# Splitting the third block's transposes around the scale sums of rows 6 to 8

## Chip, cores, metric

One core of one Trainium2 chip. The metric is the device time of one execution in microseconds (us). A profiled execution also has a span, from its first to its last instruction, which is some 1.7 us shorter. All runs that are compared are of the fast state with a granted clock of 1.0, unless the text says otherwise.

## The reference

One block of a diffusion transformer (DiT) on two batches of 256 tokens, width D = 1152, two heads of 576. What matters here is its head:

```python
mod = (_silu(c) @ w_mod).reshape(B, 6, 1, D)
shift_a, scale_a, gate_a, shift_m, scale_m, gate_m = [mod[:, i] for i in range(6)]
h = _layernorm(x, axis=-1) * (1 + scale_a) + shift_a
qkv = (h @ wqkv).reshape(B, N, 3, H, Dh)
```

Attention, the output projection and a gated MLP follow; the change doesn't touch them.

## The kernel before

The 512 tokens are four blocks of 128, numbered t = 0 to 3 in the code: "first block" is t = 0, "third block" is t = 2. VectorE normalises each block; PE transposes it in nine k-tiles (128 columns each); a k-tile is scaled by `1 + scale_a` on its way to the K projection. The scales are sums on PE over nine rows of k-tiles of `w_mod`, three rows per DMA. PE runs the units in the order of the program:

```python
def xn_T(t, ka=0, kb=KT):                      # PE: transposes of block t, k-tiles ka to kb
    ...
    for kt in range(ka, kb):
        tr(xslot(b, kt)[...], XN[:, t, kt * 128:(kt + 1) * 128], IDENT)

def sca(k0, k1):                               # PE: scale sums of rows k0 to k1, first four k-tiles
    for kt in range(k0, k1):
        mod_f0(kt)                             # two columns, bank of the first k-tile
    for kt in range(k0, k1):
        mod_kt(WSC, kt, 0, "sca_%d" % kt, (1, KC))
...
warm(7, "b")                                   # matmuls that only keep PE busy
for n, behind in ((1, "bn_ln1_1_1"), (1, "aggr_ln1_1"), (2, "veps_ln1_1"), (2, "rstd_ln1_1")):
    warm(n, behind, behind)
xn_T(1)
sca(0, 3)
warm(1, "d")
sca(3, 6)
warm(1, "f", "aggr_ln1_2")
xn_T(0)
sca(6, 9)
xn_T(2, 0, 8)
hk(0, 0)                                       # VectorE: scaled k-tile 0 for K, needs all nine rows
sc1a(0, 1, 1); sc1a(1, KC); hk(1, 0)
xn_T_copy(0, 4, 8, "act"); xn_T_copy(0, 8, 9, "act")    # ScalarE: frees two PSUM banks
...
k_first(0)                                     # PE: K projection, k-tile 0, eight matmuls
k_first(1)
xn_T(2, 8, 9)
xn_T(3)
```

## Time and profile before

| | before |
|---|---|
| time, first three runs | 244.01 us (243.94 to 244.44) |
| profiled span | 242.6 us |
| PE busy, share of the span | 98% |
| first block's transposes, sums of rows 6 to 8, third block's transposes (first matmul) | 10.19, 10.69, 11.01 us |
| K projection, k-tile 0 (first matmul); fourth block's transposes | 11.55; 13.40 us |

PE is the bound, so the change is worth what it opens or closes in PE's waits from the first block's transposes to the fourth block's. Such a wait shows as a late start of a weight load (PEld). The prediction shows and reads the lines.

### The profile page before, as it was taken

The numbers are of one execution on the slowest core, as the hardware profiler recorded it, in microseconds if no ns is written. First come the engines' busy times: TensorE is split into PE (matmuls) and PEld (weight loads), VectorE is DVE, ScalarE is ACT, GpSimd is POOL, SyncE is SP. The second block draws the span as 40 slices with busy tenths as digits, with TensorE's granted clock in tenths as the row PEclk, the third lists the DMA queues.
The fourth block names the chain that finished last, engine by engine and source line by source line (L and its number), as shares of the span: only waits on it lengthen the run. The fifth ranks groups of instructions, "written<-read, shape, count | busy, mean of one in ns | idle before, by whom it ended". The sixth has DMA issues, their size and how long they took to land.

```text
span 242.6 us, 3989 instructions
## 1 busy us (share of the span) xinstructions
PE 238.3 (98%) x1717; PEld 146.4 (60%) x1727; DVE 120.0 (49%) x216; ACT 66.9 (28%) x136; POOL 21.7 (9%) x39
## 2 busy tenths in 40 slices
PE   7999999999999999999999999999999999999996
PEld 2688854557667666898444444444565665665664
DVE  3824379596988799789999600000012222211112
ACT  4730350345424207983233332222000000000000
POOL 1500000000021186400000000020000000000000
PEclk9999999999999999999999999999999999999999
DMA  6999999999994999999943488002000000000001
GB/s 237 330 383 394 388 392 389 397 412 408 390 355 138 349 385 393 390 320 394 329 145 87 165 301 331 0 16 85 0 16 19 16 16 19 16 16 16 19 17 32
DMA packets 29995, 51.57 MB, mean 213 GB/s; under 512 B 1431, under 2 KB 15643, under 8 KB 29979
## 3 DMA queue, kind: packets, MB, share of 16 engines
q1 hardware_dynamic: 29536, 50.14, 57.8%
q0 software_dynamic: 416, 1.19, 1.6%
q8 instruction: 13, 0.21, 0.4%
q14 instruction: 3, 0.02, 0.0%
q10 hardware_dynamic: 27, 0.00, 0.0%
HBM read 50.14 MB, written 1.19 MB: 212 GB/s over the span
## 4 chain that ended last, share of the span: by engine, by line
PE 98%; issue 0%; POOL 0%; DVE 0%; POOLq 0%
PE psum L688 96%; PE psum L691 2%; POOL arena L713 0%; DVE arena L1289 0%; DVE arena L1290 0%; POOL arena L712 0%; POOL arena L719 0%; POOL arena L717 0%; POOLq L1351 0%
## 5 line engine op out<-in xcount | busy, mean ns | idle before, releaser
L688 PE MATMUL psum<-arena 128*128 128x384 bf16 (+9 forms) x1628 | 235.0, 310 | 2.0 <-POOL arena L713 1.5
L688 PEld LDWEIGHTS psum<-arena 128*128 128x128 bf16 (+1 forms) x1638 | 141.1, 97 | 91.8 <-issue 4.7
L1081 DVE SCALAR_TENSOR_TENSOR arena<-arena 128x1152 f32<-128x1152 bf16 x32 | 44.7, 1413 | 0.6
L1289 DVE TENSOR_TENSOR arena<-psum,arena 128x384 f32<-128x384 f32 (+2 forms) x13 | 6.9, 527 | 68.3 <-PE psum L688 68.3
L1197 ACT ACTIVATE arena<-psum 128x512 bf16<-128x512 f32 (+1 forms) x44 | 22.4, 519 | 42.7 <-PE psum L688 42.7
L683 ACT ACTIVATE arena<-psum 128x512 bf16<-128x512 f32 (+6 forms) x37 | 19.5, 549 | 39.8 <-PE psum L688 38.5
L685 DVE CAST arena<-psum 128x512 bf16<-128x512 f32 (+3 forms) x13 | 8.1, 639 | 11.5 <-PE psum L688 11.5
L669 POOL DMA_DIRECT2D dit_scratch<-arena x3 | 1.8, 616 | 116.4 <-DVE arena L685 59.6
L1165 POOL TENSOR_TENSOR arena<-arena 128x384 f32<-128x384 f32 x12 | 10.9, 912 | 10.9 <-DVE arena L1164 9.3
L1108 DVE CAST arena<-psum 72x32 bf16<-72x32 f32 x1 | 0.2, 188 | 21.3 <-PE psum L688 21.3
L741 DVE BATCH_NORM_STATS2 arena<-arena 128x6 f32<-128x384 f32 (+1 forms) x18 | 9.5, 551 | 0.1
L1170 ACT ACTIVATE arena<-arena 128x1152 bf16<-128x1152 f32 x4 | 5.3, 1343 | 11.3 <-DVE arena L1169 11.3
L1164 DVE TENSOR_TENSOR arena<-psum,arena 128x384 f32<-128x384 f32 x12 | 6.5, 550 | 1.3 <-PE psum L688 1.2
L691 PEld LDWEIGHTS psum<-arena 128*128 128x128 bf16 (+1 forms) x89 | 5.9, 98 | 2.1 <-DMA arena<-in_c_dram 0.8
L691 PE MATMUL psum<-arena 128*128 128x128 bf16 (+1 forms) x89 | 7.1, 219 | 0.1
L1290 DVE TENSOR_TENSOR arena<-arena 128x384 bf16<-128x384 f32 (+2 forms) x13 | 6.9, 527 | 0.4
L1187 ACT ACTIVATE arena<-psum,arena 128x128 bf16<-128x128 bf16 x16 | 6.0, 455 | 1.5 <-PE psum L691 0.9
L1184 DVE TENSOR_SCALAR arena<-psum,arena 128x128 bf16<-128x128 bf16 x20 | 5.4, 336 | 1.9 <-PE psum L691 1.9
L1085 DVE STREAM_TRANSPOSE arena<-arena 128x1152 f32<-128x1152 f32 x4 | 5.5, 1368 | 0.0
L1088 DVE TENSOR_REDUCE arena<-arena 128x36 f32<-128x1152 f32 x4 | 5.4, 1346 | 0.0
L1011 ACT ACTIVATE arena<-psum,arena 128x256 bf16<-128x256 f32 x8 | 3.7, 472 | 1.3 <-PE psum L688 0.9
L745 POOL TENSOR_TENSOR arena<-arena 128x1 f32<-128x1 f32 x6 | 3.6, 596 | 1.6 <-DVE arena L744 1.6
(48 smaller groups left out, 45.3 us busy)
## 6 DMA issues: line engine op xcount, KB each, us to landing
arena<-in_w_fc_dram SPq DMA_DIRECT2D x9, 1152.0 KB, 7.1
arena<-in_w_fc_dram SPq DMA_DIRECT2D x4, 2592.0 KB, 17.4
arena<-in_wqkv_dram SPq DMA_DIRECT2D x18, 288.0 KB, 9.7
arena<-in_w_mod_dram SPq DMA_DIRECT2D x3, 1728.0 KB, 20.5
arena<-in_w_mod_dram SPq DMA_DIRECT2D x3, 864.0 KB, 13.0
arena<-in_w_mod_dram SPq DMA_DIRECT2D x9, 288.0 KB, 11.1
arena<-in_wqkv_dram SPq DMA_DIRECT2D x1, 2592.0 KB, 16.9
arena<-in_wo_dram SPq DMA_DIRECT2D x1, 2592.0 KB, 24.4
```

Source lines behind the costliest of these rows:

```text
L683: act(c_act(n), lambda e: e.activation(out=dst, in_=src, func=ACTF.Copy), [src], [dst], name)
L685: dve(c_dve_psum16(n) if psum16 else c_dve_psum32(n), lambda e: e.tensor_copy(dst, src), [src], [dst], name)
L688: S.instr(lambda e: e.matmul(o, lhsT=l, rhs=r, start=st, stop=sp, **kw), reads=[l, r], writes=[o])
L691: S.instr(lambda e: e.transpose(o, i_, idn), reads=[i_, idn], writes=[o])
L741: dve(550, lambda e, s=s, o=o: e.bn_stats(out=o, in_=s), [s], [o], "bn_%s_%d" % (tag, ci))
L1081: dve(1270, lambda e, w=w, s=s, acc=acc: e.scalar_tensor_tensor(out=acc, in0=w, scalar=s, in1=acc, op0=ALU.mult, op1=ALU.add), [w, s, acc] ...
L1164: dve(550, lambda e, o=o, ga=ga, x1c=x1c: e.tensor_tensor(out=x1c, in0=o, in1=ga, op=ALU.mult), [o, ga], [x1c], "wo_t1_%d_%d" % (t, ci))
L1165: S.op("pool", 930, lambda e, xs=xs, x1c=x1c: e.tensor_tensor(out=x1c, in0=x1c, in1=xs, op=ALU.add), reads=[x1c, xs], writes=[x1c], name=" ...
L1187: act(440, lambda e, o=o, dst=dst, s1=s1, s2=s2: e.activation(out=dst, in_=o, func=ACTF.Identity, scale=s1, bias=s2), [o, s1, s2], [dst], ...
L1197: act(c_act(ntok), lambda e: e.activation(out=dst, in_=o, func=ACTF.Gelu_apprx_tanh), [o], [dst], "gelu_%d_%d" % (f, tok0))
L1289: dve(c_dve_psum32(w), lambda e, o=o, gm=gm, t1=t1: e.tensor_tensor(out=t1, in0=o, in1=gm, op=ALU.mult), [o, gm], [t1], "fc2_t1_%d_%d" % ( ...
L1290: dve(c_dve_32(w), lambda e, t1=t1, x1c=x1c, ost=ost: e.tensor_tensor(out=ost, in0=t1, in1=x1c, op=ALU.add), [t1, x1c], [ost], "fc2_out_%d ...
```

## The change

The intent, as far as the order tells it: let four transposes of the third block run ahead of the sums of rows 6 to 8, so that PE has something to do if the weights of those rows are late.

```diff
         warm(1, "f", "aggr_ln1_2")
         xn_T(0)
+        xn_T(2, 0, 4)
         sca(6, 9)
-        xn_T(2, 0, 8)
+        xn_T(2, 4, 8)
         hk(0, 0)
```

## The prediction

> **What bounds the kernel now.** I read the page first: the chain that ended last, then the share by engine. The tensor engine (PE) carries the whole span.
>
> ```profile
> span 242.6 us, 3989 instructions
> PE 238.3 (98%) x1717; PEld 146.4 (60%) x1727; DVE 120.0 (49%) x216; ACT 66.9 (28%) x136; POOL 21.7 (9%) x39
> ...
> PE 98%; issue 0%; POOL 0%; DVE 0%; POOLq 0%
> ```
>
> The change moves four of PE's 1717 matmuls by a few places in its order. It can therefore alter the time only by opening or closing an idle stretch of PE. The 98% can't show that, because ends of matmuls are modelled: a matmul that waits looks busy. So I read the timeline of the stretch concerned and worked with the starts of the weight loads (PEld), which do show a wait. Here is 9.7 to 14 us, where L691 is a transpose, L688 a matmul, L807 the scaling of a k-tile for the K projection, L797 the copy of the scale sums, L683 the copy of transposed tiles out of PSUM.
>
> ```profile
> 9.77 0.58 DVE L762 TENSOR_SCALAR arena<-arena 128x1152 bf16<-128x1152 bf16 x1
> ...
> 9.98 0.70 PEld L691 LDWEIGHTS psum<-arena 128*128 128x128 bf16 x9
> ...
> 10.63 0.42 PEld L688 LDWEIGHTS psum<-arena 128*128 128x128 bf16 x12
> 10.69 0.46 PE L688 MATMUL psum<-arena 128*128 128x2 bf16 x12
> 10.89 1.30 ACT L683 ACTIVATE arena<-psum 128x1024 bf16<-128x1024 bf16 x2 [1.36 <-PE psum L688]
> 10.98 0.46 PEld L691 LDWEIGHTS psum<-arena 128*128 128x128 bf16 x8
> 10.99 0.35 DVE L807 TENSOR_SCALAR arena<-psum 128x256 bf16<-128x256 bf16 x1 [0.65 <-PE psum L688]
> 11.01 0.61 PE L691 MATMUL psum<-arena 128*128 128x128 bf16 x8
> 11.27 0.22 DVE L797 COPY arena<-psum 128x2 f32<-128x2 f32 x2
> 11.52 0.35 DVE L807 TENSOR_SCALAR arena<-psum,arena 128x256 bf16<-128x256 bf16 x1
> 11.52 0.56 PEld L688 LDWEIGHTS psum<-arena 128*128 128x128 bf16 x6
> ...
> 12.24 1.04 PEld L688 LDWEIGHTS psum<-arena 128*128 128x128 bf16 x10 [0.15 <-ACT arena L683]
> ...
> 13.29 0.65 PEld L691 LDWEIGHTS psum<-arena 128*128 128x128 bf16 x10
> ```
>
> In PE's order this is: nine transposes of the first block (9.98), twelve scale sums of rows 6 to 8 (10.63), eight transposes of the third block (10.98), then the K projection, first k-tile (11.52) and second. Two things to see. PE has no hole from 9.98 to 11.44, but it has short ones at 11.52 and at 12.24. And the hole at 11.52 has no releaser, although VectorE's first scaling (10.99 + 0.35 = 11.34) had long ended. The row of the kernel's explicit waits in this stretch names it: two stand-alone waits on PE, at 11.4 and 12.4.
>
> ```profile
> L471 PEldq EVENT_SEMAPHORE  x2: 51/51/51, 11.4 to 12.4; - x2
> ```
>
> L471 is the wait on a DMA semaphore. The issues of the weights for k-tile 0 (issued 5.97) and k-tile 1 (issued 6.35), each asked for in its own narrow window, take this long to land:
>
> ```profile
> arena<-in_wqkv_dram SPq DMA_DIRECT2D x1, 288.0 KB, 5.4
> ...
> arena<-in_wqkv_dram SPq DMA_DIRECT2D x1, 288.0 KB, 6.0
> ```
>
> 5.97 + 5.4 is 11.4 and 6.35 + 6.0 is 12.4 (the trace's landing records: 11.42 and 12.39). So the first k-tile of the K projection starts when its weights land, not when VectorE is done, and the second k-tile again starts when its weights land. Between them, at 12.24, PE waits for ScalarE's second copy (10.89 + 1.30 = 12.19), since that copy frees the PSUM bank for the fourth pair of output chunks. After 12.5 us I compared each matmul's start with its column count: PE is dense nearly to the end: its holes are at most 0.13 us (the one at 20.10, behind VectorE, is of this kind), and the larger skips are single matmuls whose record is missing.
>
> **What the Trainium skill says.** "TensorE: Matmul & The Clock Gate", "Wait — 56ns, not 53.3ns?", gives 55.6 ns start to start for warm 128-column matmuls and a floor of about 25 ns for small ones. The trace agrees: the third block's eight transposes start from 11.01 to 11.39, seven steps, 55 ns each; the twelve two-column sums step by 26 ns. Switching between the two kinds adds nothing (57 ns after the last transpose, 28 ns after the last sum). "Perfetto Trace Analysis", "Sequencer-only Instruction (DRAIN, etc)", says that the reported start is the moment all semaphores are satisfied. That is how I read the wait at 11.447: the landing at 11.42 released it. The same page, "Tensor Engine Instruction (MATMUL, LD_WEIGHTS)", says the end of a matmul is an estimate; hence my use of starts.
>
> **The change part by part.** Instructions removed or added: none. The eight transposes of the third block stay eight, in the same banks (four in one bank, four in another, so the split falls on the bank border). Moved: four of them, from behind the twelve sums to ahead of them. PE's own work is the same to the nanosecond: 9x55 + 4x55 + 12x26 + 4x55. Their input is ready: the third block's normalised rows are written by 9.77 + 0.58 = 10.35, and the transposes would start at 10.63.
>
> What moves is what waits for the sums. They start 4 x 55 = 0.22 us later:
>
> 1. VectorE's first scaling reads a sum of row 8, the third of the twelve. It goes from 10.99 to 11.21 and ends at 11.57 instead of 11.35. The copies go from 11.27 to 11.49, the second scaling from 11.52 to 11.74 (end 12.09).
> 2. PE's first k-tile needs that scaling. Where PE truly waits for VectorE, at 20.10, the load starts some 0.05 us after the scaling's end (19.755 + 0.291 = 20.05). So its load would go from 11.52 to about 11.62: 0.10 us later, not 0.22, because 0.12 us were hidden behind the weights' landing.
> 3. That delay then runs into the 12.24 wait. Before: six matmuls of 256 columns (109 ns a step) from 11.555 would reach the seventh at 12.21, which waits until 12.243. After a real stall a matmul start follows the load at once, so the first starts at about 11.63 and the rest step from there after a first step of 0.12: the seventh is due at about 12.29. ScalarE's copy isn't moved (it waits for the first block's transposes alone) and ends at 12.19, so this wait vanishes. What is left of the delay: about 0.05 us; the eighth starts at 12.40 instead of 12.362.
> 4. The second k-tile starts at 12.529, as its weights land at 12.39 and the stand-alone wait and the load cost 0.14. PE would be ready for it at 12.40 + 0.11 = 12.51, and VectorE's second scaling at 12.09 + 0.05 = 12.14. So it starts at 12.529 again. Remaining delay: 0.
> 5. Everything later on PE is unchanged. The block 3 normalisation on VectorE goes from 11.79 to 12.01 (end 12.58), but its transposes start at 13.29. ScalarE's scalings wait for its own copies (12.07), not for the sums (the last copied by about 11.71).
>
> Is there a gain at the other side? The first four transposes exist 0.3 us earlier, but their consumers on VectorE and ScalarE (14.16) wait for the fourth block's transposes, at 13.29. Gain 0.
>
> Sum: +0.22 at the sums, -0.12 behind the first landing, -0.05 behind the copy, -0.05 behind the second landing: 0.0 us. Predicted 244.0, the time before.
>
> **The rivals.** *The delay stays.* If the weights land earlier in the runs that are timed than in the profiled one, steps 2 and 4 hide less. But step 3 still holds, as ScalarE's copy waits for none of the K weights: some 0.05 us would be left, 244.06. The full 0.22 (244.23) would need ScalarE's copy to be earlier too, and nothing in the profile speaks for that.
>
> *The transposes fill a DMA wait.* This is probably the intent. The scale weights of rows 6 to 8 were issued at 2.81 and took 7.7 to land, 10.5; PE comes to them at 10.63. There is a margin of some 0.13 us, so in this profile no wait to fill. If they landed 0.3 us later, PE would wait 0.17 us before and nothing after. But the K weights are behind them in the same stream and would be later too, and the second k-tile would again start at its landing. An earlier start of the sums is worth nothing then: 244.0 again, at best some 0.1 less if only that one transfer slips.
>
> *The build orders something else differently.* VectorE's and ScalarE's order is fixed by hand only up to the K projection; after that the kernel's own list scheduler picks by modelled times. A model shift of 0.2 us could swap two instructions in the softmax or the evacuations. PE is dense there and both engines have slack (VectorE 49%, ScalarE 28% busy), so I give it some 5% to matter, and then by 0.3 us either way: 243.7 to 244.3.
>
> **Range and chances.** The mechanism says 0.0 to +0.05 us. The three runs before spread from 243.94 to 244.44, ten times that, so the range is the spread of a median of such runs, with a little for the third rival: 243.6 to 244.5. Two per cent is 4.9 us; no part of this reaches a tenth of it. I leave 1% in all for the unforeseen.
>
> **What would show it right or wrong.** In the changed profile: four transposes loaded at 10.63 and four after the sums; VectorE's first scaling at 11.21; the first K load at 11.6 with VectorE's L807 as releaser, where before there was none; the wait for ScalarE's L683 at 12.24 gone or shorter; the second stand-alone wait still at 12.4; the next transposes at 13.29 as before; and the span within 0.1 us if nothing else changed. Wrong would be: the transposes at 13.29 moved by 0.1 us or more, a new wait on the second k-tile for VectorE, or another order of VectorE or ScalarE instructions after 25 us.

## The result, and the profile after

| | before | changed |
|---|---|---|
| time, six runs each | 244.07 us (243.83 to 244.44) | 244.26 us (244.23 to 244.30) |
| ratio | | 1.0007 (95%: 0.9994 to 1.002) |
| profiled span | 242.6 us | 242.6 us |

A ratio is the mean time of one kernel's fast runs over that of the other's of the same rounds, so it isn't quite the ratio of the medians quoted. Two things don't fit the prediction's picture: the medians are 0.19 us apart, and the changed kernel's six runs lie within 0.07 us, while those of the kernel before spread over 0.6 us.

The page of the changed kernel first; it answers to the first lines of the prediction.

```profile
span 242.6 us, 3999 instructions
...
PE 238.9 (98%) x1727; PEld 146.7 (60%) x1727; DVE 120.0 (49%) x216; ACT 67.0 (28%) x136; POOL 21.3 (9%) x39
```

The ten instructions more are no work: matmul records were missing from the first trace. The timeline of the stretch, changed kernel (start us, duration us, engine, line, operation; in brackets the idle time before and what ended it):

```profile
9.79 0.58 DVE L762 TENSOR_SCALAR arena<-arena 128x1152 bf16<-128x1152 bf16 x1 [0.30 <-POOL arena L745]
...
10.01 0.93 PEld L691 LDWEIGHTS psum<-arena 128*128 128x128 bf16 x13
...
10.89 0.42 PEld L688 LDWEIGHTS psum<-arena 128*128 128x128 bf16 x12
10.92 1.30 ACT L683 ACTIVATE arena<-psum 128x1024 bf16<-128x1024 bf16 x2 [1.69 <-PE psum L691]
...
11.24 0.23 PEld L691 LDWEIGHTS psum<-arena 128*128 128x128 bf16 x4
11.25 0.36 DVE L807 TENSOR_SCALAR arena<-psum 128x256 bf16<-128x256 bf16 x1 [0.87 <-PE psum L688]
...
11.66 1.64 PEld L688 LDWEIGHTS psum<-arena 128*128 128x128 bf16 x16 [0.18 <-DVE arena L807]
...
13.31 0.65 PEld L691 LDWEIGHTS psum<-arena 128*128 128x128 bf16 x10
```

As predicted there are 13 transposes, then the sums, then four transposes; the first K load waits for VectorE's L807; the wait for ScalarE (12.24 before) is gone; and the fourth block's transposes stand at 13.31 instead of 13.29. The stand-alone waits on DMA semaphores, however, moved:

```profile
L471 PEldq EVENT_SEMAPHORE  x2: 51/51/51, 11.1 to 12.3; - x2
```

The K weights landed at 11.03 and 12.00 us here, not at 11.42 and 12.39, so they hid nothing in this execution. To compare executions I use the **stretch**: from the first matmul of the first block's transposes to the first matmul of the fourth block's, on PE. It is 13.400 - 10.188 = 3.212 us before and 13.418 - 10.220 = 3.198 us after. These two profiles thus show no loss, and don't explain 0.19 us.

### The profile page after: what moved, and what is told of

Read it like the earlier page. It is cut to its first block, busy times and chain, and to the rows that moved or that the text cites. A ratio compares the mean times of both kernels' runs of the same rounds, so it can differ in the third digit from the quotient of the medians.

```text
span 242.6 us, 3999 instructions
## 1 busy us (share of the span) xinstructions
PE 238.9 (98%) x1727; PEld 146.7 (60%) x1727; DVE 120.0 (49%) x216; ACT 67.0 (28%) x136; POOL 21.3 (9%) x39
## 4 chain that ended last, share of the span: by engine, by line
PE 99%; POOL 0%; DVE 0%; issue 0%; POOLq 0%
PE psum L688 96%; PE psum L691 2%; POOL arena L713 0%; DVE arena L1290 0%; DVE arena L1291 0%; POOL arena L712 0%; POOL arena L719 0%; POOL arena L717 0%; POOLq L1352 0%
## 5 line engine op out<-in xcount | busy, mean ns | idle before, releaser
L688 PE MATMUL psum<-arena 128*128 128x384 bf16 (+7 forms) x1638 | 235.7, 311 | 1.5 <-POOL arena L713 1.5
L741 DVE BATCH_NORM_STATS2 arena<-arena 128x6 f32<-128x384 f32 (+1 forms) x18 | 9.5, 551 | 0.1
```

What stands on the lines that cost most here:

```text
L688: S.instr(lambda e: e.matmul(o, lhsT=l, rhs=r, start=st, stop=sp, **kw), reads=[l, r], writes=[o])
L741: dve(550, lambda e, s=s, o=o: e.bn_stats(out=o, in_=s), [s], [o], "bn_%s_%d" % (tag, ci))
```

## The experiments

All kernels but the three named below gave a correct result. Compared instruction by instruction, the changed kernel has the order of the kernel before on VectorE, ScalarE, GpSimd and the DMA queue; PE differs in the moved transposes alone. That removes the prediction's third rival (another order from the list scheduler) without a run.

### A control: the same kernel twice

No edit.

> The kernel before, unchanged, as a control: how much do two profiles and two sets of times of one kernel differ? I measure the stretch from the first transpose of the first block to the first transpose of the fourth block on PE (before: 10.19 to 13.40, 3.21 us; changed kernel: 10.22 to 13.42, 3.20 us). My theory (the landings of the K weights differ from run to run, by some 0.4 us between the two profiles, and the change has no part in that): ratio 1.000, and the stretch lies between 3.15 us (weights early, ScalarE's copy decides) and 3.21 us (weights as late as in the first profile). Rival (the change itself made the weights land earlier): the first K weights land again at 11.4 us, and the stretch is again 3.21.

Measured: 244.05 us (243.66 to 244.15), ratio 1.0001 (0.9987 to 1.0014). But the profiled span is 241.93 us, 0.6 us shorter than the first profile of the same kernel (242.55), and the stretch 12.777 - 9.620 = 3.157 us. The whole shift of 0.6 us exists before the first transposes. The weight loads of the first profile at the warm-up matmuls:

```profile
7.32 0.15 PEld L688 LDWEIGHTS psum<-arena 128*128 128x128 bf16 x1 [0.28 <-DVE arena L741]
7.74 0.55 PEld L688 LDWEIGHTS psum<-arena 128*128 128x128 bf16 x3 [0.28 <-issue]
8.41 0.70 PEld L691 LDWEIGHTS psum<-arena 128*128 128x128 bf16 x9
```

And of the control:

```profile
5.61 0.15 PEld L688 LDWEIGHTS psum<-arena 128*128 128x128 bf16 x1 [0.28 <-issue]
6.04 1.04 PEld L688 LDWEIGHTS psum<-arena 128*128 128x128 bf16 x5 [0.28 <-issue]
...
8.00 0.51 PEld L691 LDWEIGHTS psum<-arena 128*128 128x128 bf16 x9 [0.49 <-DVE arena L762]
...
9.42 0.69 PEld L691 LDWEIGHTS psum<-arena 128*128 128x128 bf16 x9
10.09 0.39 PEld L688 LDWEIGHTS psum<-arena 128*128 128x128 bf16 x12
10.44 0.45 PEld L691 LDWEIGHTS psum<-arena 128*128 128x128 bf16 x8
10.88 0.35 PEld L688 LDWEIGHTS psum<-arena 128*128 128x128 bf16 x4
```

(L741 is VectorE's statistics of a block, L762 its write of a block's normalised rows.) The loads one by one, 0.43 us apart, are warm-up matmuls on a half-rate clock; from 7.74 in the first profile, but from 6.04 in the control, they step by 0.22. "TensorE: Matmul & The Clock Gate", "What's actually happening", says that the clock is released after a free-running window of about 3.4 us, at a point that varies from run to run. The profiles agree: their clock records put the release between 4.92 and 7.81 us. I call a release early where PE has finished its warm-ups before VectorE has written the second block's rows, and late otherwise. With a late release PE is still busy with warm-ups when VectorE has the second block ready, and its transposes start at 8.6; with an early one PE waits for VectorE (0.49 us in the control) and they start at 8.0. From there on PE is 0.6 us earlier, **but VectorE is not**. It writes the third block's rows (the L762 after that) by 10.39 in the control and by 10.35 in the first profile. (Over all kept profiles these rows are written between 10.35 and 10.64 us, with either kind of release: later where the input landed later, 10.39 for a landing at 4.58, 10.63 for one at 4.82.) Both profiles that the prediction and its check rested on had a late release.

The first K weights landed at 10.78 in the control, in an unchanged kernel: the change has no part in their landing.

### Doses: four again, eight, two transposes ahead

```diff
-        xn_T(0)
+        xn_T(0); xn_T(2, 0, 4)                # four_again: the change, line numbers kept
         sca(6, 9)
-        xn_T(2, 0, 8)
+        xn_T(2, 4, 8)
```

In `two_ahead` the split is at k-tile 2, in `eight_ahead` all eight go ahead of the sums.

> The changed kernel (its two calls on one line, so that line numbers stay those of the kernel before). Theory: the delay of 0.22 us at the sums is nearly all hidden, the first K load waits for VectorE and comes 0.05 us after its end, the wait for ScalarE's second copy at 12.24 is gone, stretch 3.19 to 3.21 us whatever the landings, ratio 1.000. Rival (the delay stays in full): stretch 3.43 and ratio 1.001, as the 0.19 us between the medians suggests.

> All eight transposes of the third block ahead of the sums, twice the dose. Theory: the sums and VectorE's first scaling come 0.44 us later than before (scaling 11.43 to 11.79), the first K load at 11.84, and now the 0.3 us that this is late exceed what ScalarE's copy (0.05) and the second landing (0.06) hide: stretch 3.40 us, span and time 0.2 us longer (ratio 1.0008). Rival (the position of the transposes doesn't matter, VectorE is never waited for): stretch 3.21, ratio 1.000. Rival (the delay is proportional): twice whatever the four cost.

> Two transposes ahead, half the dose. Theory: VectorE's scaling comes 0.11 us later and ends at 11.46, PE's first K load at about 11.52, where it was before: no new wait. Stretch 3.15 to 3.21 us, ratio 1.000. If the delay were passed on in proportion, half of what the four cost.

| | time us | ratio | stretch us |
|---|---|---|---|
| four_again | 244.27 (244.17 to 244.33) | 1.0008 (0.9995 to 1.0021) | 3.563 |
| eight_ahead | 244.49 (244.28 to 244.86) | 1.0018 (1.0005 to 1.0030) | 3.786 |
| two_ahead | 244.23 (243.99 to 244.73) | 1.0009 (0.9996 to 1.0023) | 3.414 |

All three expectations of the stretch failed: 3.19 to 3.21, 3.40, 3.15 to 3.21. The doses don't start from zero either: even two transposes cost 0.26 us of stretch against the control. The loads of four_again say why:

```profile
9.55 0.66 PEld L691 LDWEIGHTS psum<-arena 128*128 128x128 bf16 x9
10.58 0.23 PEld L691 LDWEIGHTS psum<-arena 128*128 128x128 bf16 x4 [0.36 <-DVE arena L762]
10.76 0.41 PEld L688 LDWEIGHTS psum<-arena 128*128 128x128 bf16 x12
11.11 0.23 PEld L691 LDWEIGHTS psum<-arena 128*128 128x128 bf16 x4
11.53 1.64 PEld L688 LDWEIGHTS psum<-arena 128*128 128x128 bf16 x16 [0.19 <-DVE arena L807]
```

and, of the same kernel, VectorE's write of the third block's rows:

```profile
9.94 0.58 DVE L762 TENSOR_SCALAR arena<-arena 128x1152 bf16<-128x1152 bf16 x1
```

The clock was released early here (at 5.01). PE has finished the first block's transposes and comes to the moved ones 0.36 us before VectorE has written their rows (9.94 + 0.58 = 10.52). PE runs in order, so the sums, whose weights have landed (10.08), wait behind them. In the kernel before, the sums go first and this wait of PE doesn't exist.

### The transposes in the same place, with rows that are ready

```diff
-        xn_T(0); xn_T(2, 0, 4)
+        xn_T(0); xn_T(2, 0, 4, 1)             # reads the second block's rows: a wrong result on purpose
```

> The changed order, but the four moved transposes read the second block's rows, which are ready since 8 us (a wrong result on purpose; number, kind and place of the instructions as in the changed kernel). New theory: when PE's clock is released early, PE reaches the moved transposes before VectorE has written the third block's rows and waits 0.36 us for them, with the sums stuck behind. Then this kernel has no such wait: stretch 3.20 us (3.157 of the unchanged kernel plus what is left of the 0.22 us), against 3.56 of four_again, and times like the kernel before (ratio 1.0002, spread as wide as before's 0.4 us, lowest run near 243.7). Rival (the cost is the place of the transposes, whatever they read): stretch 3.56, ratio 1.0008, all runs between 244.2 and 244.3.

Measured: 244.10 us (243.88 to 244.61), ratio 1.0001 (0.9988 to 1.0013), stretch 13.055 - 9.857 = 3.198 us, with an early release (5.12). The thirteen transposes run without a hole:

```profile
9.31 0.41 PEld L688 LDWEIGHTS psum<-arena 128*128 128x128 bf16 x13 [0.41 <-DMA arena<-in_w_mod_dram]
9.64 0.93 PEld L691 LDWEIGHTS psum<-arena 128*128 128x128 bf16 x13
10.53 0.42 PEld L688 LDWEIGHTS psum<-arena 128*128 128x128 bf16 x12
...
11.29 1.64 PEld L688 LDWEIGHTS psum<-arena 128*128 128x128 bf16 x16 [0.18 <-DVE arena L807]
```

The stretch is the expected 3.20 and not the rival's 3.56, and the times spread again, by 0.7 us. The lowest run, 243.88, isn't quite at the 243.7 that I had named. So the place of the transposes as such doesn't cost 0.41 us. The test is weaker than planned, though: in this execution PE waited 0.41 us for the scale weights of rows 3 to 5 (the load at 9.31) and came to the moved transposes only at 10.36, and VectorE wrote the third block's rows at 10.37. Even with these rows PE would have waited only some 0.07 us, an estimate from these numbers. That it is the wait for the rows that costs rests on the traces that show this wait (four_again above, early_four and trim_four below): there the stretch grows by the length of the wait.

### K weights early: does a landing hide the delay?

```diff
-            for k0, k1 in ((0, 3), (3, 6), (6, 9)):
+            for k0, k1 in ((0, 3), (3, 6), (6, 9))[:2 + (ka > 0)]:
```

The first-chunk sums of rows 6 to 8 take rows 3 to 5 (a wrong result). `early_four` adds the change.

> The order of before, with the K weights early: the first load of the scale weights' rows 6 to 8 (384 KB) is left out and sums 6 to 8 of the first chunks take rows 3 to 5 instead (a wrong result on purpose; it passes the check of races and memory). All later loads move up by about 1 us, so the first K weights land near 10.4 and the second near 11.4. Theory: the first K load comes right behind the last transpose (step 57 ns instead of 162), then ScalarE's two copies are waited for, the second k-tile follows at once; stretch 3.15 us.

> The same early K weights with the change (wrong result on purpose, as in early_before). Theory: the landings can't hide anything now, only ScalarE's copy does: stretch 3.19 us, 0.04 us more than early_before of the same call. Rival (the delay of 0.22 us, or its visible 0.1, was hidden by the landings alone): 0.10 to 0.22 us more. Rival (no delay at all): the same stretch.

Measured: early_before 243.61 us (243.53 to 243.82), stretch 3.156, the first two K weights landed at 9.77 and 10.43, even earlier than expected; early_four 244.16 us (244.12 to 244.18), stretch 3.563. The first is what the theory said, and it is also the control's stretch, so in an early-release execution of the kernel before the landings decide nothing. The second isn't: 0.41 us more instead of 0.04, again with 0.36 us of waiting for L762 ahead of the moved transposes. All four runs of one are 0.30 to 0.65 us above all four of the other. Not all of that need be the change: in the two profiles VectorE's rows differ too (10.35 in early_before, 10.63 in early_four), as the input landed at 4.18 and 4.82 us.

### Two warm-up matmuls fewer

If the release of the clock makes the kernel before spread, and VectorE pins the changed one, then a shorter warm-up queue should help the former alone.

```diff
-        for n, behind in (..., (2, "veps_ln1_1"), (2, "rstd_ln1_1")):
+        for n, behind in (..., (2, "veps_ln1_1")):
```

> The kernel before without the last two warm-up matmuls (those behind the second block's reciprocal root); correct result. If a late release of PE's clock is what makes the kernel before spread (the warm-up matmuls still take 0.43 us each and the first transposes start at 8.6 instead of 8.0), then the queue ends 0.4 us earlier in those runs: the slow ones (244.3 to 244.4) fall to 243.9 to 244.2, the fast ones stay at 243.7; ratio 0.999. Rival (the later landings of the K weights bound such runs anyway): ratio 1.000. Risk: the clock is released one window later and the runs get slower by up to 1.7 us.

> The changed kernel without the same two warm-up matmuls; correct result. New theory: it is pinned by VectorE's third block whatever PE does before, so an earlier PE gains nothing: 244.2 to 244.3 as four_again, spread 0.15 us, ratio 1.0008, and the wait of the moved transposes for VectorE's L762 is there. Rival (the change only costs where the clock comes early): it falls with trim_before.

Measured: trim_before 243.84 us (243.67 to 244.09) against 244.13 us (243.73 to 244.47), ratio 0.9987 (0.9975 to 0.9999); trim_four 244.25 us (244.02 to 244.32), ratio 1.0002 (0.9990 to 1.0014), with the wait in its trace:

```profile
10.69 0.23 PEld L691 LDWEIGHTS psum<-arena 128*128 128x128 bf16 x4 [0.27 <-DVE arena L762]
```

trim_before came out as the new theory said. trim_four did in part: the wait is there and the median is as expected, but the ratio is 1.0002 instead of 1.0008, and the runs spread by 0.30 us instead of 0.15. trim_before is the one correct version whose median lies below both kernels, by 0.3 us; its interval just excludes 1, which for one of thirteen comparisons is weak. Its profile had an early release (4.92; stretch 3.156), so what it does in a late one is inferred from its times, not seen; the danger of a release one window later didn't show in five runs.

### Rows 6 to 8 late: the case that the change is meant for

```diff
+                if k0 != 3 or ka: continue    # the first K weights go ahead of the scale weights of rows 6 to 8
+                dma(WK[:, 0, :], wqkv_v[:, 0, D:2 * D], P * D * 2, "ld_wk0", run=2304)
```

> The order of before, with the scale weights of rows 6 to 8 late: the first K weights (288 KB) are issued ahead of them, after the input has landed, so these rows land near 11.4 instead of 10.5 and PE has a real wait ahead of the sums, the case the change is meant for. Correct result. Theory: PE waits from 10.64 to 11.45 at the sums, then transposes to 12.2, first K load at 12.2, stretch about 3.78 us.

> The change on top of late_before: four transposes now lie in the wait. Theory: the K projection can't start before the sums, their copy through VectorE's scaling and its signal, about 0.67 us from the first sum to the first K load; before, the sums and eight transposes took 0.76 us. So of the 0.22 us moved into the wait only 0.1 us is gained: stretch 3.67 us. Rival (the transposes fill the wait in full): 0.22 us less than late_before, 3.56. Rival of the prediction (nothing is gained, as the next landing decides): the same 3.78.

> late_before once more, as its first profile fell in an execution with a throttled clock (0.993) and its three other runs (244.46 to 244.98) overlap those of late_four (244.26 to 245.0). Theory: PE waits at the sums for the rows 6 to 8 (landing 10.8 to 12.1), and the change can gain at most 0.1 us there: 244.75, less than 0.2 us over late_four's 244.59. Rival (the transposes fill the wait in full): 0.3 us over late_four or more.

Inconclusive. The landing of rows 6 to 8 scattered: 12.09 us in late_before, 11.35 in late_before_again, and 10.83 in late_four, where PE came to the sums at 10.89 and had nothing to wait for (stretch 3.198, as the changed kernel without the edit). late_before_again did wait, and its stretch of 3.761 us is close to the 3.78 expected of late_before. The fast runs at full clock are 244.46 to 244.98 (late_before), 243.77 to 245.07 (late_before_again) and 244.26 to 245.00 (late_four): they overlap. (The ratios, 1.0050, 1.0059 and 1.0022, compare with the unedited kernel, and the first two mix in the executions at half rate named below.) So whether the split gains where PE really waits for these rows stays open, and the expected 0.1 us isn't shown. late_before_again allows an estimate: its sums were 0.74 us late, for which the line fitted to the changed order below gives a stretch of 3.72 us, so the split would have saved some 0.04 us of its 3.761.

One thing came out beside it. In late_before PE waited 1.88 us for the rows, and its clock fell to half. The windows of that kernel (from and to in us, length, busy us of PE, PEld, DVE, ACT and POOL with counts, granted clock, DMA share, GB/s):

```profile
10.00:12.00 2.00, 0.43 (x8) 0.26 (x5) 0.57 (x2) 1.30 (x2) 0.87 (x1) 0.98 1.00 283
12.00:13.00 1.00, 0.86 (x18) 0.86 (x19) 0.53 (x4) 0.00 (x0) 0.00 (x0) 0.50 1.03 375
...
15.00:16.00 1.00, 1.00 (x9) 0.87 (x8) 0.00 (x0) 0.00 (x0) 0.00 (x0) 0.84 1.07 376
```

From 11.9 to 15.3 us PE ran at half rate. That execution (246.94 us) and three of late_before_again's (246.54 to 246.89, clock 0.993) are left out above.

## Why the prediction was right, and where it was not

The time was right: 244.0 predicted, 244.26 measured, range 243.6 to 244.5. The mechanism was half right. "Delay" below is how much longer it is from the first block's first transpose to the first sum than the 0.50 us of the kernel before.

| kernel | release of the clock us | delay of the sums us | stretch us |
|---|---|---|---|
| before, first profile | 7.76 | 0 | 3.212 |
| before, control | 6.19 | 0 | 3.157 |
| early_before | 6.0 to 6.3 | 0 | 3.156 |
| trim_before | 4.92 | 0 | 3.156 |
| changed, first profile | 7.81 | 0.22 | 3.198 |
| four_ready | 5.12 | 0.22 | 3.198 |
| late_four | 7.71 | 0.22 | 3.198 |
| two_ahead | 5.6 to 5.8 | 0.44 | 3.414 |
| trim_four | 6.0 to 6.4 | 0.49 | 3.469 |
| four_again | 5.01 | 0.59 | 3.563 |
| early_four | 7.01 | 0.59 | 3.563 |
| eight_ahead | 5.65 | 0.81 | 3.786 |

(Where the trace has no clock record, the release lies between the last warm-up step of 0.43 us and the first shorter one.) Every kernel of this table with a delay fits one line: stretch = 3.157 + delay - 0.18 us, within 5 ns. So the head of the kernel has 0.18 us of slack behind the sums, and what exceeds it is paid in full.

- **Steps 1 and 2** held: the sums came 0.22 us later in the profile of the changed kernel, and the first K load waited for VectorE's scaling and came at 11.66 (11.62 predicted).
- **Step 3** held: the wait for ScalarE's copy vanished, and "some 0.05 us" were to remain; 3.198 - 3.157 = 0.041 us remained.
- **Step 4**, the landing that hides the rest, holds for the first profile alone. In that execution it had stretched the kernel before by 3.212 - 3.157 = 0.055 us. In the control and in the changed kernel's profile the weights landed earlier and hid nothing.
- **The step that failed** is the sentence ahead of step 1: "Their input is ready: the third block's normalised rows are written by 9.77 + 0.58 = 10.35, and the transposes would start at 10.63." That margin of 0.28 us was one execution's. PE's arrival moves by 0.6 us with the release of its clock, and VectorE's rows don't move with it. With an early release the moved transposes wait for them, the delay is 0.59 us instead of 0.22, and 0.41 us of stretch is paid against the control. four_ready, which has ready rows, pays 0.04 (though its PE also came later, as said above).
- **The spread** of 243.94 to 244.44 was taken for noise, and part of it is not. To set VectorE's own shifts aside, count from the end of its write of the second block's rows to the fourth block's first transpose. With a late release this is 5.48 us in both orders (the two first profiles). With an early one it is 4.80 to 4.88 us in the order before (control, early_before, trim_before), but 5.20 us in the changed order (four_again, early_four and trim_four, within 1 ns). So an early release saves 0.6 to 0.7 us in the order before and only 0.28 us in the changed one, where VectorE's rows then decide; with a late one PE comes to the moved transposes 0.29 us after these rows would let it go (10.72 against 10.43). The difference in the medians, 0.19 us both times, fits a loss in the executions with an early release, but the timed ratios (intervals from 0.9994 and 0.9995 up) don't show it. Nor is the small spread of the changed kernel explained: its eleven runs (first six and four_again) all lie between 244.17 and 244.33, but those of eight_ahead and two_ahead, which wait for the same rows, spread over 0.58 and 0.74 us.
- **Rivals.** "The delay stays" named the right size for what is left without landings (0.05 us), and missed the new wait. "The transposes fill a DMA wait" had nothing to fill in any profile of the kernel as given or changed: those rows had landed by 9.97 to 10.48 us, ahead of PE. Another order of the other engines did not occur.

## What to carry to other kernels

An instruction moved forward in an in-order engine carries its own wait with it, and blocks what was behind it; check when its input is ready against the earliest, not the profiled, arrival of the engine. Where one engine's clock is released at a time that varies and the other engines keep their times, one profile shows one of several interleavings: profile the unchanged kernel twice, and take a spread in its times as a question. A margin behind an instruction (0.18 us here) is worth measuring by doses, as only the excess over it costs.

## What the Trainium skill lacked or had wrong

- "TensorE: Matmul & The Clock Gate", Part 1, says that the release of the clock varies with a free-running window, by 500 ns either way, and that the ramp matters little. Here it varied by 2.9 us (4.92 to 7.81) over eleven profiles with a clock record. (The same section also lets the count of slow matmuls of one kernel vary from 6 to 14, which is nearer to this; and its bound of 1% of the span for the ramp holds here.) The page lacks that the release shifts PE against VectorE, which kept its times (rows written by 10.35 and 10.39 us in the two profiles of the kernel before), and so changes which wait binds: 0.6 us of PE's position at the first transposes, and a wait of 0.36 us that is there or not.
- The same page, "Why this matters for your kernels", advises against gaps of PE above about 3 us. In late_before's profile, the only trace of this kind, the clock fell at 11.90, 1.7 us after the start of PE's last matmul ahead of a wait of 1.88 us, and stayed at half until 15.31 us; a shorter one of about 0.7 us (late_before_again's profile) did no harm.
- The same page, "PE-mode transpose", says that the full clock doesn't engage for transposes. Here the kernel's transposes followed the granted clock: 55 ns from start to start at full rate, 107 ns in late_before at half rate. Whether transposes alone would release it, no run shows.
